# Sketched attention with a tanh-shrink layer on one core: key and query projections and the fold in larger matmuls, weights cast on other engines

## The chip, the core and the metric

The kernel runs on one core of a Trainium2 chip. Its engines run side by side, each with its own queue in program order: TensorE (PE; the loading of its weights, PEld, has a row of its own in the profile), VectorE (DVE), ScalarE (ACT), GpSimd (POOL) and SyncE (SP), which here only issues transfers. The metric is the device time of one execution in microseconds (us). A smaller number is better.

## The reference, cut to what matters

```python
# q, k, v: (4 batches, 4 heads, 1088 tokens, 32), S1, S2: (8, 32)
def phi(x):                                # 64 features for a token
    a = einsum('rd,bhsd->bhsr', S1, x)
    b = einsum('rd,bhsd->bhsr', S2, x)
    return (a[..., :, None] * b[..., None, :]).reshape(*x.shape[:-1], 64)
q_p, k_p = phi(q), phi(k)
kv = einsum('bhsf,bhsd->bhfd', k_p, v)
z = k_p.sum(axis=2)
num = einsum('bhsf,bhfd->bhsd', q_p, kv)
den = einsum('bhsf,bhf->bhs', q_p, z)[..., None] + 1e-06
x = (num / den)   # heads side by side: (4352 tokens, 128)
h = x @ w_in      # w_in: (128, 2048)
out = (h - tanh(h)) @ w_out               # w_out: (2048, 128)
```

## The kernel before, in words

**Planner.** The body does not issue instructions. `Program.op` (L74) records an operation with its engine, an assumed cost, the buffers it reads and writes, a priority and, for PE, a `mode` (which tile shape of the array it uses) and a count `ni` of instructions. `schedule` (L128) lists the operations in an order for each engine, `sync` (L226) puts the semaphore waits in, and `emit` (L290) writes the five queues. So the constants at L31 to L48, the costs and the priorities decide the order in which each engine takes its work; a wait at the head of a queue holds up all that stands behind it.

**Attention, batch by batch.** The first batch is cut into a chunk `a` of 512 tokens and a chunk `c` of 576; the others are one chunk each. The steps of a batch, with the lines of the profile:

- keys are loaded (L449) and turned by DVE (L547); PE projects them on both sketches (L565: for each 128 tokens two float32 matmuls of 64 tokens each, mode `k`); ACT and DVE copy them out (L575); POOL and DVE multiply out the 64 features (L583, L590);
- PE sums features times values, one 32-column tile for a head (L616), and a small Gram matrix of the sketches (L606), both in mode `kv`; DVE masks the Gram matrix (L634), PE folds S1 and S2 into it (L642, eight float32 matmuls in 32-column tiles), and the result goes beside the query sketch in `wq` (L649), so that the denominator comes out of the query projection; the sums are spread, turned and stored as `ndw` (L653, L659, L664);
- queries are loaded and turned (L465, L671); PE projects them (L700: four matmuls of 64 rows by 64 tokens for each 128 tokens, mode `q`); DVE goes through the denominator, its reciprocal and the products (L712 to L733, with POOL's half at L728) and turns the features (L739); PE weighs them with `ndw` in 32x32 tiles (L754, mode `nd`); DVE writes the result as bfloat16 into `xT` (L766, L772).

**Layer.** For each group of 512 tokens (eight, and a last one of 256), 16 times: PE multiplies `xT` by a 128-column block of `w_in` (L838), ACT takes tanh(-h) out of PSUM into a slot of `tt` (L841, 56 slots), PE adds tt times a block of `w_out` to an accumulator (L849). The linear term h @ w_out is x times the product w_in @ w_out, which is made once (L797, L802, L809, L813, L814) and added as a high and a low bfloat16 part (L830). DVE turns the accumulator (L856) and SP issues four transfers for each piece of the output (L865).

**Opening.** `load_w_in` and `load_w_out` are issued on SP straight behind the first batch's loads (L469, L473), in float32. `casts` makes them bfloat16: one quarter of `w_in` on ACT, three on POOL, both halves of `w_out` on POOL (L781, L786). `warm` (L510) gives PE matmuls on a zero tile to fill its gaps until the first chunk has been weighed. What sets the order around the change: SP's queue (k, v, q, then weights, then the next batch behind gates), ACT's queue up to the first tanh, and PE's queue, in which L797, L700 of chunk c and L754 of chunk a stand between the sums and the first L838. The gates at L39 name the step of a batch after which the next batch's k, q and v loads may be issued.

Of the kernel before, what the change touches and what calls it, by code (L numbers as in the profile page):

```python
# [12 lines left out]
R = 8  # L13
# [20 lines left out]
COPY_K = ("scalar", "scalar", "vector")  # L34
COPY_U = "vector"
COPY_Z = "scalar"
COPY_W = "scalar"
W_PRIO = 14
GATES = "kab", "x", "qp"  # L39
# [3 lines left out]
STRETCH = {"tensor": 1.3, "scalar": 1.3, "vector": 3, "gpsimd": 1.3, "sync": 1}  # L43
PASSES, HOLD, HELD = 6, 1.3, ("vector",)
FILL = 0.6
WARM = 4000
PACKET, FETCH, AHEAD = 256, 4500, 56
# [3 lines left out]
class Op:  # L51
    __slots__ = ("ni", "want", "eng", "cost", "fn", "deps", "order", "prio", "sem", "mode", "kids", "need", "ready", "at", "end", "idx", "know", "waits", "inc", "val")

    def __init__(self, eng, cost, fn, prio, sem, mode, want, ni):
        self.want, self.ni = want, ni
# [8 lines left out]
class Program:  # L64


    def __init__(self, nc):
        self.nc = nc
        self.ops = []
        self.writer = {}  # L70
        self.readers = {}
        self.last_fill = None

    def op(self, eng, cost, fn, r=(), w=(), prio=None, sem=None, mode=None, want=None, ni=2):  # L74
# [17 lines left out]
        for k in r:  # L92
            if k not in w:
                self.readers.setdefault(k, []).append(o)
        self.ops.append(o)
# [8 lines left out]
    def rank(self):  # L104
# [14 lines left out]
        for o in reversed(topo):  # L119
# [5 lines left out]
            if o.prio is None:  # L125
                o.prio = t / 1000
# [11 lines left out]
    def listed(self, seen):  # L138
# [21 lines left out]
        count, packets = 0, [0, 0]  # L160
# [11 lines left out]
        while left:  # L172
            best = None
            for e in engines:
# [3 lines left out]
                o = min((o for o in avail[e] if when(o) <= t + 20), key=lambda o: (o.prio, o.idx))  # L178
# [4 lines left out]
            fill = o.prio == 5000  # L183
# [12 lines left out]
            if o is self.last_fill:  # L196
                rest = [x for x in avail[e] if x.prio == 5000]
                left -= len(rest)
                avail[e] = [x for x in avail[e] if x.prio != 5000]
            o.at = when(o)  # L200
            dma = o.sem is not None
            if e == "tensor":
                if o.mode != mode:
                    o.at, mode = o.at + MODE, o.mode
                if (count + AHEAD) // PACKET != (count + o.ni + AHEAD) // PACKET:
                    packets.append(o.at + FETCH)
                count += o.ni
            cost = o.cost * 2 if e == "tensor" and o.at < WARM else o.cost
            if dma:
                bus = max(bus, o.at + 1500) + o.cost  # L210
                free[e], o.end = o.at + ISSUE, bus + 500
# [133 lines left out]
def bass_polysketch_attn__then__act_tanh_shrink_kernel(nc, q, k, v, S1, S2, moe_w_in, moe_w_out, out):  # L345
# [22 lines left out]
    pmask = sb("pmask", [128, 2])  # L368
    bmask = sb("bmask", [128, H])
    cmask = sb("cmask", [128, H])  # L370
    s_raw = sb("s_raw", [16, D])
    sel = sb("sel", [16, 16, R])
    s2c = sb("s2c", [128, H, D])
    wkm = sb("wkm", [128, 2, H, R])
    wq = sb("wq", [128, B, 2, 24])
# [3 lines left out]
    qT = [sb(f"qT{i}", [128, S]) for i in range(2)]  # L379
# [16 lines left out]
    w_out_f = sb("w_out_f", [128, NJB, DM])  # L396
# [45 lines left out]
    def load_small():  # L442
        load("scalar", 1024, ("s_raw",), "s", -3000, lambda e: e.dma_start(out=s_raw[0:8, :], in_=S1), True)
        load("scalar", 1024, ("s_raw",), "s", -3000, lambda e: e.dma_start(out=s_raw[8:16, :], in_=S2), True)
# [23 lines left out]
    def load_w_in(x, prio):  # L468
        load("sync", 262144, ("w_in_f", x), f"wi{x}", prio, lambda e: e.dma_start(  # L469
            out=w_in_f[:, 512 * x:512 * x + 512], in_=moe_w_in[:, 512 * x:512 * x + 512]))  # L470

    def load_w_out(x, prio):
        load("sync", 524288, ("w_out_f", x), f"wo{x}", prio, lambda e: e.dma_start(  # L473
            out=w_out_f[:, 8 * x:8 * x + 8, :].rearrange("p (x j) c -> p x (j c)", x=2),
            in_=moe_w_out.rearrange("(x ji jb) c -> ji x (jb c)", x=4, jb=4)[:, 2 * x:2 * x + 2, :]))


    def constants():
# [9 lines left out]
        for i in range(2):  # L488
            P.op("gpsimd", 100, lambda e, i=i: e.memset(kT[i][:, 8, 2:4, :], 0.0), w=[("kT0", i)], prio=-2980)
        P.op("gpsimd", 150, lambda e: e.memset(vx[0][64:128, :, 8, :], 0.0), w=[("vx0", 0)], prio=-2970)  # L490
# [3 lines left out]
        for r in range(2):  # L494
# [5 lines left out]
            out=pmask[:, :], in0=hmask[:, 0:2], in1=hmask[:, 2:4], op=ALU.add), r=[("hmask",)], w=[("pmask",)], prio=-2800)  # L500
        P.op("gpsimd", 150, lambda e: e.tensor_copy(
# [459 lines left out]
```

## Time and profile before

| | us |
|---|---|
| three runs | 115.69, 117.2, 121.72 |
| median of the runs | 117.2 |
| the profiled execution, device time | 114.97 |
| its span in the profile | 113.2 |
| PE busy / weight loads / DVE / ACT / POOL | 98.3 / 53.3 / 60.4 / 78.2 / 26.3 |
| first tanh starts | 20.98 |
| last tanh phase (no batch left to prepare) starts | 84.66 |
| last PE matmul group (L849 x16) starts | 107.22 |
| last DVE turn ends, then the last transfers | 109.68 |

PE's 3165 recorded rows (1573 matmuls and 1592 weight loads) come from its instruction stream; a float32 matmul leaves two matmul rows and two weight-load rows, a bfloat16 one leaves one of each. The granted clock is 1.0 in every stretch. In a row of the timeline the columns are start, length, engine, line, operation, output and inputs, count, and in brackets the idle time before it and what ended it; "issue" means that the profile shows nothing that it waited for.

### The profile page before, as it was taken

Reading aid. Unit: us, or ns where it says so; the run is one execution under the profiler, and the core shown is the slowest. Engines: PE = TensorE matmul, PEld = TensorE weight load, DVE = VectorE, ACT = ScalarE, POOL = GpSimd, SP = SyncE. Lnnn points to the kernel's source line nnn. Section 1 sums busy time; section 2 is a strip of 40 time slices with the busy share of each in tenths; the row PEclk is TensorE's granted clock in tenths of the full one; section 3 lists DMA queues with packets and bytes.
Section 4 is the critical chain, followed back from the end, with each engine's and each line's share of the span. In section 5 each row is a group of like instructions: output and inputs, shape, how many; then the busy total and the mean of one; then the engine's idle time right before and its main releaser. Section 6 shows DMA issues by size and latency. Waiting matters only on the chain.

```text
span 113.2 us, 3618 instructions
## 1 busy us (share of the span) xinstructions
PE 98.3 (87%) x1573; PEld 53.3 (47%) x1592; DVE 60.4 (53%) x115; ACT 78.2 (69%) x160; POOL 26.3 (23%) x34
## 2 busy tenths in 40 slices
PE   5999195699999996898999999799999999989950
PEld 2467174265556442546643464564444434435540
DVE  4677722997637996639399374739953020020210
ACT  4021251987766980797599669749979999999900
POOL 6352796400710150260025007002400000000000
PEclk9999999999999999999999999999999999999999
DMA  3988999300420505991000657060004114014062
GB/s 101 278 229 249 322 414 254 87 10 0 97 112 0 93 3 163 155 335 41 6 0 6 176 99 212 6 97 1 0 12 69 18 19 73 0 26 67 0 96 46
DMA packets 23663, 11.24 MB, mean 99 GB/s; under 512 B 18784, under 2 KB 21344, under 8 KB 23648
## 3 DMA queue, kind: packets, MB, share of 16 engines
q1 hardware_dynamic: 23616, 11.02, 38.7%
q8 instruction: 12, 0.20, 0.7%
q14 instruction: 3, 0.02, 0.1%
q10 hardware_dynamic: 32, 0.00, 0.0%
HBM read 8.78 MB, written 2.23 MB: 97 GB/s over the span
## 4 chain that ended last, share of the span: by engine, by line
PE 61%; ACT 11%; DVE 10%; DMA 7%; issue 6%; DVEq 0%
PE ps L849 16%; PE ps L838 15%; ACT tt L841 10%; PE ps L754 7%; PE ps L512 5%; PE ps L700 5%; DMA kraw<-in_k_dram 4%; DMA qraw<-in_q_dram 3%; PE ps L565 3%; PE ps L830 3%; DVE qpT L739 2%; PE ps L616 2%; DVE osb L856 2%; DVE qp L733 1%; PE ps L659 1%
## 5 line engine op out<-in xcount | busy, mean ns | idle before, releaser
L841 ACT ACTIVATE tt<-ps 128x512 bf16<-128x512 f32 (+1 forms) x144 | 70.0, 598 | 11.5 <-PE ps L754 6.6
L838 PE MATMUL ps<-xT,w_in 128*128 128x512 bf16 (+1 forms) x133 | 45.5, 368 | 3.4 <-DVE xT L766 1.1
L849 PE MATMUL ps<-tt,w_out 128*128 128x512 bf16 (+1 forms) x139 | 42.0, 367 | 0.2 <-issue 0.2
L838 PEld LDWEIGHTS ps<-xT,w_in 128*128 128x128 bf16 x144 | 13.1, 97 | 20.7 <-ACT tt L841 8.0
L849 PEld LDWEIGHTS ps<-tt,w_out 128*128 128x128 bf16 x144 | 14.1, 98 | 13.5 <-ACT tt L841 1.0
L856 DVE STREAM_TRANSPOSE osb<-ps 128x512 f32<-128x512 f32 (+1 forms) x9 | 6.1, 674 | 21.4 <-PE ps L849 15.0
L728 POOL TENSOR_TENSOR qp<-an,ab 128x1152 f32<-128x1152 f32 (+2 forms) x5 | 8.9, 1777 | 27.0 <-DVE an L724 26.8
L583 POOL TENSOR_TENSOR wk<-kab 128x512 f32<-128x512 f32 (+1 forms) x8 | 9.4, 1180 | 22.8 <-DVE kab L575 19.5
L739 DVE STREAM_TRANSPOSE qpT<-qp 128x1152 f32<-128x1152 f32 (+2 forms) x10 | 11.0, 1119 | 0.7 <-POOL qp L728 0.6
L754 PE MATMUL ps<-qpT,ndw 32*32 32x288 f32 (+3 forms) x320 | 7.3, 353 | 1.7 <-issue 1.2
L766 DVE CAST xT<-ps 128x512 bf16<-128x512 f32 x8 | 5.2, 682 | 5.8 <-PE ps L754 5.8
L512 PE MATMUL ps<-wz 128*128 128x512 bf16 x17 | 6.3, 484 | 1.7 <-DVE hmask L484 1.2
L671 DVE STREAM_TRANSPOSE qT<-qraw 128x512 f32<-128x512 f32 (+3 forms) x9 | 5.6, 658 | 4.0 <-DMA qraw<-in_q_dram 3.9
L547 DVE STREAM_TRANSPOSE kT<-kraw 128x256 f32<-128x256 f32 (+3 forms) x10 | 6.0, 612 | 3.0 <-DMA kraw<-in_k_dram 2.9
L616 PE MATMUL ps<-wk,vx 128*32 128x64 f32 x288 | 5.4, 221 | 2.4 <-issue 2.4
L754 PEld LDWEIGHTS ps<-qpT,ndw 32*32 32x32 f32 x320 | 4.2, 103 | 4.3 <-issue 1.7
L590 DVE TENSOR_TENSOR wk<-ps,kab 128x512 f32<-128x512 f32 (+1 forms) x8 | 5.7, 748 | 0.8 <-ACT kab L575 0.7
L700 PEld LDWEIGHTS ps<-wq,qT 64*64 64x64 f32 x320 | 5.2, 135 | 1.7 <-DVE wq L649 0.7
L700 PE MATMUL ps<-wq,qT 64*64 64x48 f32 (+2 forms) x320 | 5.9, 220 | 0.0
L616 PEld LDWEIGHTS ps<-wk,vx 128*32 128x32 f32 x288 | 4.4, 110 | 2.6 <-issue 2.5
L733 DVE TENSOR_TENSOR qp<-an,ps 128x1152 f32<-128x1152 f32 (+2 forms) x5 | 5.6, 1113 | 0.2
L575 ACT COPY kab<-ps 128x320 f32<-128x320 f32 (+1 forms) x5 | 2.1, 415 | 5.1 <-PE ps L565 5.0
(64 smaller groups left out, 66.2 us busy)
## 6 DMA issues: line engine op xcount, KB each, us to landing
kraw<-in_k_dram SPq DMA_DIRECT2D x3, 544.0 KB, 4.5
qraw<-in_q_dram SPq DMA_DIRECT2D x3, 544.0 KB, 4.1
out_dram<-osb SPq DMA_DIRECT2D x20, 64.0 KB, 2.0
w_in_f<-in_moe_w_in_dram SPq DMA_DIRECT2D x4, 256.0 KB, 5.0
w_out_f<-in_moe_w_out_dram SPq DMA_DIRECT2D x2, 512.0 KB, 8.3
vx<-in_v_dram SPq DMA_DIRECT2D x6, 144.0 KB, 3.0
vx<-in_v_dram SPq DMA_DIRECT2D x6, 128.0 KB, 3.3
vx<-in_v_dram SPq DMA_DIRECT2D x6, 64.0 KB, 2.7
```

The lines of the kernel that those rows point to most:

```text
L512: P.op("tensor", cost, lambda e: e.matmul(ps[:, 6, :], wz[:, 0:128], wz[:, :], start=True, stop=True), r=[("wz",)], prio=prio)
L583: P.op("gpsimd", pool(64 * n), lambda e, t0=t0, t1=t1, n=n, ab_=ab_: e.tensor_tensor(out=wk[:, 1, t0:t1, :, :].rearrange("p t h (i j) -> p ...
L616: ins = e.matmul(ps[32 * h:32 * h + 32, 2, 0:64], vx[i][:, h, t, :], wk[:, h // 2, t, h % 2, :], start=(t == 0), stop=(t == 8), tile_posit ...
L700: ins = e.matmul(dst[:, :, y0:y1], qT[i][64 * r:64 * r + 64, x:x + 64], wq[64 * r:64 * r + 64, b, :, y0:y1], start=True, stop=True, tile_p ...
L728: P.op("gpsimd", pool(64 * n), lambda e: e.tensor_tensor(out=qp[u][:, 1, 0:64 * n].rearrange("p (n i j) -> p n i j", i=R, j=R), in0=an[u][ ...
L733: P.op("vector", dve(64 * n), lambda e: e.tensor_tensor(out=qp[u][:, 0, 0:64 * n].rearrange("p (n i j) -> p n i j", i=R, j=R), in0=an[u][: ...
L739: P.op("vector", dve(64 * n), lambda e, r=r: e.transpose(out=qpT[u][:, r, 0:64 * n], in_=qp[u][:, r, 0:64 * n]), r=[("qp", u, r)], w=[("qp ...
L754: ins = e.matmul(ps[32 * h:32 * h + 32, k0 + s, 0:32 * own[s]], ndw[b % 2][32 * s:32 * s + 32, y, 32 * h:32 * h + 32], src, start=(y == 0) ...
L838: P.op("tensor", pe(n), lambda e, jb=jb, bk=bk: e.matmul(bk[:, 0:n], w_in[:, 128 * jb:128 * jb + 128], xT[:, t0:t0 + n], start=True, stop= ...
L841: P.op("scalar", act(n), lambda e, ts=ts, bk=bk: e.activation(out=tt[:, ts, 0:n], in_=bk[:, 0:n], func=AF.Tanh, scale=-1.0), r=[kb], w=[(" ...
L849: P.op("tensor", pe(n), lambda e, jb=jb, ts=ts: e.matmul(acc[:, 0:n], w_out[:, jb, :], tt[:, ts, 0:n], start=(jb == 0 and not g), stop=(jb ...
L856: P.op("vector", dve(n), lambda e: e.transpose(out=osb[u][:, 0:n], in_=acc[:, 0:n]), r=[ka], w=[("osb", u)], want=due(NJB) + LAG)
```

## The change

Parts on the data path:

1. **Projections and fold.** The key projection takes 128 tokens as one weight tile (9 matmuls a batch, 64 columns out, no tile position) where it took two of 64. The query projection takes 128 tokens: in the first batch with all 128 rows at once (`whole`, 96 columns out, a masked copy `wqb` of the sketch), in the others in two halves of 64 rows by 128 tokens (`halves`). The fold is two matmuls with 128 columns where it was eight with 32, and the sketch itself is spread with one matmul where it took four, S1 and S2 being loaded four times side by side for that. `qT` gets 64 zeroed columns.
2. **w_out** is loaded by two transfers on POOL's own queue that cast to bfloat16 on the way, behind POOL's product of chunk a; its float32 buffer and its two casts on POOL are gone, and its rows lie in another order (rows of 512 bytes in HBM).
3. **w_in** is issued on SP only after the first Gram matrix has been masked (`gm`); its four casts are all on ACT, with the same order of columns on both sides.
4. **Opening x** of chunk a is copied out of PSUM by ACT instead of DVE; the two `w_inT` copies go from ACT to DVE, and these turns of `w_in` use banks 0 and 2.
5. **Small moves.** In the later batches both key copies and the copy of the folded sketch are on ACT. The last group's four output transfers are issued two by SP and two by ACT. Gram and sums of the later batches are two operations. The first fill of PE is 40 matmuls of 64 columns, then 512-column ones. The q and v loads of the next batch have earlier gates.
6. **Planner.** Other constants, an instruction-fetch model with another start, and a rule that PE stays in a tile mode while it has work in it. So the order in every queue differs.

The diff, cut to its core:

```diff
-COPY_K = ("scalar", "scalar", "vector")
-COPY_U = "vector"
+COPY_K = ("scalar", "scalar", "scalar")
+COPY_U = "scalar"
-COPY_W = "scalar"
-W_PRIO = 14
-GATES = "kab", "x", "qp"
+COPY_W = "vector"
+W_PRIO = 30
+W_IN = -600, -599
+W_OUT = 9, 9
+BURN = 40
+X_A = "scalar"
+GATE_IN = ("gm",)
+GATE_OUT = ("qp", 0, 1)
+GATES = "kab", "qp", "an"
...
-STRETCH = {"tensor": 1.3, "scalar": 1.3, "vector": 3, "gpsimd": 1.3, "sync": 1}
-PASSES, HOLD, HELD = 6, 1.3, ("vector",)
+STRETCH = {"tensor": 1.3, "scalar": 1.3, "vector": 2.2, "gpsimd": 1.6, "sync": 1}
+PASSES, HOLD, HELD = 6, 0.6, ("vector",)
...
-PACKET, FETCH, AHEAD = 256, 4500, 56
+PACKET, FETCH, SLOW, BUSY = 256, 3200, 4500, 18000
...
-                o = min((o for o in avail[e] if when(o) <= t + 20), key=lambda o: (o.prio, o.idx))
+                o = min((o for o in avail[e] if when(o) <= t + 20), key=lambda o: (e != "tensor" or mode is None or o.mode != mode, o.prio, o.idx))
...
+    def load_w_in():
+        for x in range(4):
+            load("sync", 262144, ("w_in_f", x), f"wi{x}", W_IN[x // 2], lambda e, x=x: e.dma_start(
+                out=w_in_f[:, 512 * x:512 * x + 512], in_=moe_w_in[:, 512 * x:512 * x + 512]), gate=GATE_IN)
+            P.op("scalar", act(512) + 60, lambda e, x=x: e.copy(
+                w_in[:, 512 * x:512 * x + 512], w_in_f[:, 512 * x:512 * x + 512]),
+                r=[("w_in_f", x)], w=[("w_in", x)], prio=C_PRIO)
+
+    def load_w_out():
+        for x in range(2):
+            load("gpsimd", 524288, ("w_out", x), f"wo{x}", W_OUT[x], lambda e, x=x: e.dma_start(
+                out=w_out[:, 8 * x:8 * x + 8, :],
+                in_=moe_w_out.rearrange("(j p) c -> p j c", p=128)[:, 8 * x:8 * x + 8, :]), gate=GATE_OUT)
...
+        P.op("vector", dve(64), lambda e: e.tensor_tensor(
+            out=wqb[:, :, :, 0:16], in0=acc[:, None, None, 0:16].to_broadcast([128, 2, 2, 16]),
+            in1=hmask[:, :].rearrange("p (r h) -> p h r", h=2)[:, :, :, None].to_broadcast([128, 2, 2, 16]), op=ALU.mult),
+            r=[ka, ("hmask",)], w=[("wab",)])
...
                 for t in range(t0, t1):
-                    for c in range(2):
-                        ins = e.matmul(dst[64 * c:64 * c + 64, :, :, t - t0, :],
-                                       kT[i][:, t, 2 * c:2 * c + 2, :].rearrange("p c j -> p (c j)"),
-                                       wkm[:, :, :, :].rearrange("p x h i -> p (x h i)"),
-                                       start=True, stop=True, tile_position=(0, 64 * c))
+                    ins = e.matmul(dst[:, :, :, t - t0, :], kT[i][:, t, :, :].rearrange("p c j -> p (c j)"),
+                                   wkm[:, :, :, :].rearrange("p x h i -> p (x h i)"), start=True, stop=True)
...
             for y in range(2):
-                for h in range(H):
-                    ins = e.matmul(ps[32 * h:32 * h + 32, gb, 64:80], s2c[:, h, :],
-                                   gm[:, 2 * y:2 * y + 2, :].rearrange("p h i -> p (h i)"), start=(y == 0), stop=(y == 1),
-                                   tile_position=(0, 32 * h))
+                ins = e.matmul(ps[:, gb, 64:80], s2c[:, :, :].rearrange("p h d -> p (h d)"),
+                               gm[:, 2 * y:2 * y + 2, :].rearrange("p h i -> p (h i)"), start=(y == 0), stop=(y == 1))
...
+            def whole(e):
+                for t in range(nt):
+                    x = 32 * c.c0 + 128 * t
+                    dst = ps[:, k0, 96 * t:96 * t + 96].rearrange("p (h y) -> p h y", h=4)
+                    ins = e.matmul(dst[:, :, y0:y1], qT[i][:, x:x + 128],
+                                   wqb[:, :, :, y0:y1].rearrange("p h r y -> p (h r) y"), start=True, stop=True)
                 return ins
+            def halves(e):
+                for t in range(nt):
+                    x = 32 * c.c0 + 128 * t
+                    for r in range(2):
+                        dst = ps[:, k0 + r, 48 * t:48 * t + 48].rearrange("p (h y) -> p h y", h=2)
+                        ins = e.matmul(dst[:, :, y0:y1], qT[i][64 * r:64 * r + 64, x:x + 128],
+                                       wq[64 * r:64 * r + 64, b, :, y0:y1], start=True, stop=True,
+                                       tile_position=(64 * r, 0))
+                return ins
+            return halves if b else whole
...
-            P.op("vector", dve(128 * (z - a)), lambda e, a=a, z=z: e.tensor_copy(
+            eng = X_A if c.x == 0 else "vector"
+            P.op(eng, (dve if eng == "vector" else act)(128 * (z - a)), lambda e, a=a, z=z, eng=eng: (e.tensor_copy if eng == "vector" else e.copy)(
...
-                P.op("sync", 128 * w / 250, lambda e, b=b, c=c, m=m, cb=cb, at=done: e.dma_start(
+                P.op("scalar" if g == len(groups) - 1 and cb % 2 else "sync", 128 * w / 250, lambda e, b=b, c=c, m=m, cb=cb, at=done: e.dma_start(
...
-    warm(60, 216, 5000)
+    warm(BURN, 64, 29, 4999)
+    warm(60, 512, 216, 5000)
...
-    for x in range(4):
-        load_w_in(x, -790)
-    load_w_out(0, -760)
-    load_w_out(1, -750)
     sketch()
-    casts()
...
     k_back(0, a)
-    q_front(a, 0, early=True)
+    load_w_in()
+    q_front(a, 1, early=True, ab_eng=AB_A)
+    load_w_out()
```

## The prediction, as it was put on record

> **What bounds the kernel now.** I read the page's busy shares first, then the chain, then the timeline of ACT, because the layer's 144 tanh are all there.
>
> ```profile
> PE 98.3 (87%) x1573; PEld 53.3 (47%) x1592; DVE 60.4 (53%) x115; ACT 78.2 (69%) x160; POOL 26.3 (23%) x34
> ...
> q8 instruction: 12, 0.20, 0.7%
> ...
> PE 61%; ACT 11%; DVE 10%; DMA 7%; issue 6%; DVEq 0%
> ```
>
> PE has most of the chain, but 6% of it, some 7 us, is "issue". ACT's timeline:
>
> ```profile
> 20.98 2.56 ACT L841 ACTIVATE tt<-ps 128x512 bf16<-128x512 f32 x5
> ...
> 45.91 1.57 ACT L841 ACTIVATE tt<-ps 128x512 bf16<-128x512 f32 x3 [3.82 <-PE ps L754]
> ...
> 84.66 18.61 ACT L841 ACTIVATE tt<-ps 128x512 bf16<-128x512 f32 x38 [0.81 <-PE ps L754]
> ```
>
> There are three stages. Up to 20.98 nothing of the layer runs. From there to 84.66 ACT starves whenever the next batch's x is late (3.82 before batch 1's, at 45.91): the chain of a batch (keys, sums, queries, DVE, weighing) sets the pace, with PE nearly full. From 84.66 ACT is full at 18.61/38 = 0.49 a tanh. PE's timeline says why the first stage is long:
>
> ```profile
> 13.62 0.41 PE L616 MATMUL ps<-wk,vx 128*32 128x64 f32 x11 [2.37 <-issue]
> ...
> 19.07 0.41 PE L754 MATMUL ps<-qpT,ndw 32*32 32x128 f32 x4 [1.19 <-issue]
> ```
>
> PE stops twice in the middle of one operation, with data there. Counting PE's rows in its order, matmuls and weight loads, 442 lie ahead of the first stop and 255 between the two. Queue q8 brought 12 packets for about 3,200 rows. So I read the stops as instruction fetches of 256 rows that are late: if each is asked for when the one before is entered, the two took 13.62 - 8.65 = 5.0 and 19.07 - 13.62 = 5.45.
>
> **The change part by part.**
>
> *Fetches.* With the new order, 428 rows stand ahead of the first weighing. The edge at 442 falls into its first half, the edge at 698 into chunk c's weighing at about 23. A fetch asked for at row 186 (about 9.0) is in by 14.5, and the weighing starts at 15.3. Both stops go; what covers the fetch is 0.8 us.
>
> *Price of a 128-column float32 weight tile.* This is the largest unknown. The rows of the shapes replaced, and the one row of a full float32 tile (L659, a transpose):
>
> ```profile
> 46.23 1.13 PEld L565 LDWEIGHTS ps<-wkm,kT 128*64 128x64 f32 x36 [0.42 <-DVE xT L766]
> ...
> 52.90 0.22 PEld L642 LDWEIGHTS ps<-gm,s2c 128*32 128x32 f32 x16 [0.69 <-DVE gm L634]
> ...
> 53.14 0.20 PEld L659 LDWEIGHTS ps<-ident,kvz 128*128 128x128 f32 x2
> ```
>
> One L565 load lasts 0.138 and one of L659 0.14, so the starts are (1.13 - 0.138)/35 = 0.028 apart, and the chain shows 1.20 for the 36 rows, 0.033 each. In L659 the second load starts 0.20 - 0.14 = 0.06 after the first. Lower bound: 64 columns stream in 0.053 (two L565 rows, side by side, take 0.056 to 0.066). Upper bound: columns per ns fall with the number of column tiles, 32/0.0073 with four (L642: (0.22 - 0.112)/15), 64/0.028 with two; halved again, one full tile takes 0.111. I take 0.066, twice L565's row, because L659 is the only row of the shape itself. Then a key projection is 18 x 0.066 = 1.19 against 1.20; queries (two row tiles side by side) 36 x 0.033 = 1.19 against 1.24 (L700); the fold 4 x 0.066 = 0.26 against 0.25. So no gain and no loss. The Trainium skill (TensorE: Matmul & The Clock Gate, LDWEIGHTS) says that a weight load takes its columns divided by 1.2 GHz, whatever the rows, and that its fast load leaves out float32. That is 0.107 for 128 columns: it speaks against this change and for the upper bound, and by it the sum is that of rival 1.
>
> *Opening, walked along the new queues with the durations of the trace.* The sketch arrives at 4.28 as before. The 40 short fills must be over by then: at 0.06 each from 1.19 they are (L809 runs 16 matmuls in 0.89, 0.056 each); at half the clock, seen in 0.43 for a 512-column fill, 0.11 each, they would cost 1.7. PE: key projection 5.95 to 6.5 and 6.9 to 7.6, four fills, Gram 8.8, sums 9.4, a/b projection 9.9, fold 10.2, four fills, second projection 11.6, chunk c's 10 rows of 96 columns at 0.085 to 12.4, second sums 13.0. DVE: an is ready 1.3 after 11.75 (as from 10.75 to 12.03), qpT at 14.8 and 15.8. ACT: chunk c's copy until 12.9, then casts and copies in turn (cast, kvz 0.38, cast, ndw 0.37, cast, cast). A cast took 1.09 with scattered columns; with columns in order I take 0.6, the tanh of the same shape, so w_in is ready at 16.05. Its four transfers start at 9.3 instead of 6.38; the first quarter took 4.6 in a busy queue, so 13.9 at worst, 1.0 behind ACT's place for it, and this is in the range. PE: first turn of w_in 15.2, weighing 15.3 to 16.4, second turn 16.85. The x copy on ACT (0.37 for 256 columns, 0.42 for 320, so 0.57) ends at 17.1, the first tanh starts at 17.65: 3.3 earlier. With casts at 1.09 it would be 19.2. The two w_inT copies cost DVE 1.2 each (1.35 for 1152 columns) and are covered: chunk c's features are ready at 21.4, its weighing comes at about 23.
>
> *What reaches batch 1.* PE now needs nine tanh and the product ahead of chunk c's weighing: that ends at 24.5 and the key projection at 26.95, against 29.00: 2.0 earlier. The other 1.3 is lost again, as ACT waits for batch 1's x.
>
> *Batches.* Key projection and fold no longer switch the tile mode: four switches less a batch at about 0.1 (L565 starts 0.09 behind its turn at 27.73): 0.4 x 3 = 1.2. Two waits go: the mask of Gram stood behind a key turn that waited for its transfer (0.69 idle ahead of L642 at 52.90, above), 0.6; and batch 3's queries were late:
>
> ```profile
> 71.23 1.37 DVE L671 STREAM_TRANSPOSE qT<-qraw 128x576 f32<-128x576 f32 x2 [2.15 <-DMA qraw<-in_q_dram]
> ```
>
> Their gate now opens at the turned features instead of xT, so 1.0 of this comes back (the sums ended at 72.2, the projection began at 74.11). The copies moved to ACT, 0.37 + 0.17 a batch, lie in its starved time; without that cover 1.6.
>
> *Tail.* The last four output transfers take SP some 0.45 each behind the last turn; with two on ACT 0.8 is saved.
>
> *w_out.* Its 2.2 of casts on POOL go. The first transfer is issued behind POOL's product, at 14.2. PE's queue stops for it at the first L849, at 19.5, and for the second at the product, at 21.3; behind both stand all L838, so ACT starves too. No row shows a transfer issued by POOL. Lower bound: SP's issue, 0.45; upper: 8.3 for each, w_out's own time to landing now. With k, q and w_out, 2.15 MB at the 0.39 MB/us of 14 to 18 us, the second lands near 20.7. I take no stall.
>
> Sum against the profiled execution: 2.0 + 1.2 + 0.6 + 1.0 + 0.8 = 5.6, so 114.97 - 5.6 = 109.4. That execution lies 1.9% below the median of the runs (117.2), of which it would leave 111.6. I forecast 111.0, between the two.
>
> **The rivals.**
>
> 1. *Full float32 tiles load at 0.111.* For: the fall from four column tiles to two. Against: L659. Each batch gets 18 x 0.045 = 0.8 for keys, 36 x 0.023 = 0.8 for queries, 0.2 for the fold, in a chain that ACT waits for: 5.3 in three batches; the opening's 16 + 18 + 10 such rows add 1.9. Time 109.4 + 7.2 = 116.6, on the median's scale 118.8: slower than before. It decides from 0.101 a row, where 5.6 is used up.
> 2. *w_out late.* At 8.3 for each, one behind the other, the second lands at 30.8, 9.5 behind its place: 118.9. It overturns the gain from a landing at 26.9. For: POOL's queue makes 1,024 short rows for each transfer and its next product waits behind; against: the same queues moved 0.41 MB/us in 14 to 16. The Trainium skill (DMA: Bandwidth & Descriptors, Anatomy of one DMA) gives a POOL-issued transfer 2.0 us plus bytes over 436 GB/s, 3.2 for 0.5 MB, an estimate that no run here shows yet; by it there is no stall.
> 3. *The opening keeps its stops.* The fetch takes 7.8, as the k load did in that stretch, and PE stops for 1.4 in the weighing, or the fills or casts cost their upper bounds. The first tanh is at 19.1 to 19.4 and batch 1's chain gains some 0.5 instead of 2.0: 110.9, on the median's scale 113.1.
>
> **How the numbers follow.** Forecast 0.60, rival 1 0.17, rival 2 0.10, rival 3 0.13. Low end: PE's work from the first L838 at 17.2 is about 82.3 (272 full L838 and L849 at 0.2157 make 58.7, the linear part 3.7, weighing 6.0, sums and Gram 4.1, keys 3.6, queries 3.6, product, turns and folds 2.6); with 2.5 for the switches left and 114.97 - 109.14 - 0.8 = 5.0 behind the last matmul this gives 107.0, and with float32 rows at 0.053 1.7 less, 105.3. High end: 118.8 and 118.9 of the rivals. About 2% can be told from no change in this kernel. Faster by more: the forecast less 0.02 and most of rival 3, 0.68; within 2%: much of rival 1, 0.18; slower: 0.14, rival 2 and the rest of rival 1.
>
> **What would show it.** No idle row of PE marked "issue" above 0.5 up to 20; first tanh between 17 and 18.5; a key projection of 1.1 to 1.3 in the chain (2.0 means rival 1); w_out landing by 19.5 and 21.3; 45.91 at about 44; at most 0.5 of waiting for qraw. I am wrong if the full tiles cost over 0.1 a row or the first L849 waits for a transfer.

## The result, and the profile after

The changed kernel takes 124.65 us in the median of six runs (121.78 to 131.27); the kernel before, beside it, 117.76 (115.69 to 123.33). The ratio, taken over the undisturbed runs of both, is 1.0485, with a 95% interval of 1.0368 to 1.0602: the change makes the kernel slower by some 5%, and the forecast of 111.0 us was wrong. Times of both kernels spread by several us, mainly through their opening, so I compare profiles by stretches. The profiled execution of the changed kernel takes 121.78 us (span 120.0, before 113.2). First the lines of its page that answer to those shown of before: the busy time of the engines, the granted clock of TensorE in tenths over 40 slices of 3 us, two transfer queues, and the chain's shares.

```profile
PE 107.8 (90%) x1304; PEld 64.8 (54%) x1320; DVE 59.8 (50%) x113; ACT 79.8 (67%) x167; POOL 23.2 (19%) x33
...
PEclk9999999967999999999999999999999999999999
...
q0 software_dynamic: 2080, 0.52, 4.6%
q8 instruction: 10, 0.16, 0.7%
...
PE 72%; DMA 9%; DVE 9%; ACT 3%; issue 2%; POOL 1%; ACTq 0%; DVEq 0%
```

PE has 541 rows less and is 9.5 us busier; transfers went from 7% to 9% of the chain, issue from 6% to 2%; and the clock, 1.0 throughout before, dips around 25 us. ACT's timeline of the changed kernel, columns as before:

```profile
19.08 3.05 ACT L866 ACTIVATE tt<-ps 128x512 bf16<-128x512 f32 x6 [0.48 <-PE ps L820]
24.40 1.72 ACT L866 ACTIVATE tt<-ps 128x512 bf16<-128x512 f32 x3 [2.27 <-PE ps L863]
28.54 1.57 ACT L866 ACTIVATE tt<-ps 128x512 bf16<-128x512 f32 x3 [2.42 <-PE ps L863]
...
50.90 1.57 ACT L866 ACTIVATE tt<-ps 128x512 bf16<-128x512 f32 x3 [4.78 <-PE ps L786]
...
91.95 18.68 ACT L866 ACTIVATE tt<-ps 128x512 bf16<-128x512 f32 x38 [0.93 <-PE ps L786]
```

The first tanh is 1.9 earlier (19.08 against 20.98). Batch 1's tanh, at 45.91 before, comes at 50.90; the last phase, at 84.66 before, at 91.95. So a lead of 1.9 has become a lag of 5.0 within one batch, and grows by 2.3 in the next two. PE's timeline and the chain of waits show two causes:

```profile
16.82 1.15 PE L786 MATMUL ps<-qpT,ndw 32*32 32x128 f32 x64
...
23.54 0.60 PE L874 MATMUL ps<-tt,w_out 128*128 128x512 bf16 x2 [2.44 <-DMA w_out<-in_moe_w_out_dram]
...
26.34 1.87 PE L834 MATMUL ps<-w_out,w_inT 128*128 128x128 bf16 x16
```

```profile
31.60 1.96 PE ps L588 x18
...
37.90 0.55 PE ps L660 x4
...
39.11 2.17 PE ps L730 x36
```

The chain of waits of the kernel before has these rows for the same steps of batch 1 (L565 keys, L642 fold, L700 queries):

```profile
27.80 1.20 PE ps L565 x36
...
34.20 0.25 PE ps L642 x16
...
35.04 1.24 PE ps L700 x72
```

The weighing (L786) runs through where L754 stopped for 1.19. At 21.1 PE is ready for w_out and waits 2.44 us; the product (L834), whose row lasts 1.06 before, takes 1.87. And the wide tiles of batch 1 take 1.96 for keys (18 rows), 2.17 for queries (36) and 0.55 for the fold (4), where the chain before had 1.20, 1.24 and 0.25 to 0.32: 0.109, 0.060 and 0.14 a row.

### The profile page after: what moved, and what is told of

It is laid out like the page before. It is cut to its first block, busy times and chain, and to the rows that moved or that the text cites. A ratio compares the mean times of both kernels' runs of the same rounds, so it can differ in the third digit from the quotient of the medians.

```text
span 120.0 us, 3074 instructions
## 1 busy us (share of the span) xinstructions
PE 107.8 (90%) x1304; PEld 64.8 (54%) x1320; DVE 59.8 (50%) x113; ACT 79.8 (67%) x167; POOL 23.2 (19%) x33
## 3 DMA queue, kind: packets, MB, share of 16 engines
q0 software_dynamic: 2080, 0.52, 4.6%
## 4 chain that ended last, share of the span: by engine, by line
PE 72%; DMA 9%; DVE 9%; ACT 3%; issue 2%; POOL 1%; ACTq 0%; DVEq 0%
PE ps L874 20%; PE ps L863 20%; PE ps L588 7%; DMA w_out<-in_moe_w_out_dram 6%; PE ps L730 5%; PE ps L786 5%; ACT tt L866 3%; PE ps L855 3%; PE ps L637 3%; DMA s_raw<-in_S_dram 3%; PE ps L537 2%; DVE qpT L771 2%; PE ps L660 2%; DVE osb L881 2%; PE ps L834 2%
## 5 line engine op out<-in xcount | busy, mean ns | idle before, releaser
L874 PE MATMUL ps<-tt,w_out 128*128 128x512 bf16 (+1 forms) x142 | 42.8, 371 | 2.6 <-DMA w_out<-in_moe_w_out_dram 2.4
L863 PEld LDWEIGHTS ps<-xT,w_in 128*128 128x128 bf16 x144 | 13.7, 101 | 19.9 <-ACT tt L866 7.2
L588 PEld LDWEIGHTS ps<-wkm,kT 128*128 128x128 f32 x72 | 8.7, 192 | 1.0 <-DVE xT L800 0.6
L588 PE MATMUL ps<-wkm,kT 128*128 128x64 f32 x72 | 8.7, 273 | 0.0
L537 PE MATMUL ps<-wz 128*128 128x64 bf16 (+1 forms) x57 | 7.2, 287 | 1.5 <-DVE hmask L504 1.2
L596 ACT COPY kab<-ps 128x256 f32<-128x256 f32 (+1 forms) x8 | 3.2, 399 | 7.0 <-PE ps L588 7.0
L786 PE MATMUL ps<-qpT,ndw 32*32 32x288 f32 (+3 forms) x320 | 6.9, 352 | 0.9 <-DVE qpT L771 0.9
L744 DVE COPY ab<-ps 128x576 f32<-128x576 f32 (+1 forms) x4 | 2.7, 674 | 8.3 <-PE ps L730 7.5
L800 DVE CAST xT<-ps 128x512 bf16<-128x512 f32 x7 | 4.6, 687 | 4.5 <-PE ps L786 4.5
L730 PEld LDWEIGHTS ps<-wq,qT 64*128 64x128 f32 x108 | 6.3, 188 | 0.8 <-ACT wq L673 0.4
L730 PE MATMUL ps<-wq,qT 64*128 64x48 f32 x108 | 6.6, 274 | 0.0
L786 PEld LDWEIGHTS ps<-qpT,ndw 32*32 32x32 f32 x320 | 4.0, 103 | 3.6 <-DVE qpT L771 1.8
```

The source lines that it names most:

```text
L537: P.op("tensor", cost, lambda e: e.matmul(ps[:, 6, 0:cols], wz[:, 0:128], wz[:, 0:cols], start=True, stop=True), r=[("wz",)], prio=prio)
L588: ins = e.matmul(dst[:, :, :, t - t0, :], kT[i][:, t, :, :].rearrange("p c j -> p (c j)"), wkm[:, :, :, :].rearrange("p x h i -> p (x h i) ...
L730: ins = e.matmul(dst[:, :, y0:y1], qT[i][64 * r:64 * r + 64, x:x + 128], wq[64 * r:64 * r + 64, b, :, y0:y1], start=True, stop=True, tile_ ...
L786: ins = e.matmul(ps[32 * h:32 * h + 32, k0 + s, 0:32 * own[s]], ndw[b % 2][32 * s:32 * s + 32, y, 32 * h:32 * h + 32], src, start=(y == 0) ...
L863: P.op("tensor", pe(n), lambda e, jb=jb, bk=bk: e.matmul(bk[:, 0:n], w_in[:, 128 * jb:128 * jb + 128], xT[:, t0:t0 + n], start=True, stop= ...
L874: P.op("tensor", pe(n), lambda e, jb=jb, ts=ts: e.matmul(acc[:, 0:n], w_out[:, jb, :], tt[:, ts, 0:n], start=(jb == 0 and not g), stop=(jb ...
```

## The experiments

The table gives, for the profile of each run, the first tanh and the stretch from there to the end of the span. The second number depends little on how fast the opening ran, except where PE waits for w_out or its clock falls behind a wait. "Wide" and "narrow" are the tiles of batches 1 to 3; "late" is w_out's place in the changed kernel.

| kernel | first tanh | from there to the end |
|---|---|---|
| before | 20.98 | 92.2 |
| before, profiled again (e13) | 23.40 | 92.8 |
| before with wide tiles (e10) | 21.71 | 97.2 |
| before with 42 rows more (e11) | 21.59 | 92.3 |
| after: wide, late | 19.08 | 100.9 |
| e1: narrow, late | 24.88 | 98.9 |
| e2: wide, early | 25.00 | 96.7 |
| e3: wide, late, wait filled | 24.45 | 100.4 |
| e4: narrow, early | 29.55 | 92.0 |
| e5: wide, late, fills ahead | 18.73 | 105.5 |
| e8: as e5, opening narrow | 18.07 | 109.2 |
| e6, e7: narrow, early, fills ahead | 20.34, 23.11 | 95.1, 91.9 |
| e9: wide, late in 2 KB rows, fills ahead | 20.49 | 98.1 |
| e14: all narrow, late, fills ahead | 17.97 | 96.3 |
| e12: all narrow, earliest, fills ahead | 19.14 | 91.7 |

**The wide tiles.** My theory: they load at 0.11 a row and lie on the path. The rival: w_out alone did it. `e1_narrow_batches` undoes the tiles where b is not 0 (cut to its core; the fold likewise):

```diff
+NARROW = lambda b: b > 0
...
+                    for c in range(2 if NARROW(b) else 0):
+                        ins = e.matmul(dst[64 * c:64 * c + 64, :, :, t - t0, :],
...
+                    if NARROW(b):
+                        continue
...
-                    for r in range(2):
...
+                    for s, r in [(s, r) for s in range(2) for r in range(2)]:
...
-                                       tile_position=(64 * r, 0))
+                                       tile_position=(64 * r, 64 * s))
```

> The changed kernel, but in batches 1 to 3 the key projection is again two tiles of 64 columns, the query projection four of 64 by 64, and the fold eight of 32 columns; every instruction keeps its place, and the opening keeps its wide tiles. Theory A (the wide float32 tiles are loaded at 0.11 us and lie on the path): key rows of a batch go from 1.96-2.04 us back to about 1.2, query rows from 2.15 to about 1.25, fold from 0.55 to about 0.3, so some 1.9 us a batch; chunk c's weighing stays at 29.3, batch 1's tanh after x at 50.9 moves to about 49, the last phase from 91.95 to 86-88, the span from 120.0 to 115-116. Rival B (w_out's late landing alone; the wide tiles lie in time that TensorE would wait anyway): the rows shrink as much, but the span stays within 119-120.5.

`e10_before_wide` does the one part alone in the kernel before (the same lines the other way round):

> The kernel before with only one part of the change: in batches 1 to 3 the key projection in tiles of 128 columns, the query projection in tiles of 64 by 128 (the last of nine left narrow), and the fold in one of 128 columns; each instruction group in its old place. Theory A (a 128-column float32 load costs 0.11 against 0.066 for two of 64 columns, and lies on the path): +1.7 to 1.9 us a batch, last phase at 89.8-90.4 instead of 84.66, span 118.3-119 against 113.2. Rival B (in the old order there is slack that takes it): span 113-115.5.

ACT's timeline of e1, the tanh that follow on the x of batches 1, 2 and 3:

```profile
58.45 1.57 ACT L880 ACTIVATE tt<-ps 128x512 bf16<-128x512 f32 x3 [4.78 <-PE ps L877]
...
76.70 2.07 ACT L880 ACTIVATE tt<-ps 128x512 bf16<-128x512 f32 x4 [1.11 <-PE ps L877]
...
95.74 18.69 ACT L880 ACTIVATE tt<-ps 128x512 bf16<-128x512 f32 x38 [0.93 <-PE ps L877]
```

The steps are 18.25 and 19.04, against 20.13 and 20.92 after: 1.88 less each, as expected. The span as such (123.8, times 117.89 to 125.56) says nothing, since this profile's opening ran at half speed and w_out made PE wait 4.76; both are taken up below. In e10 the stretch behind the first tanh grows by 5.0, one step from 19.37 to 21.31, the next from 19.38 to 20.68, one from 24.93 to 26.64. Its times give only 1.0199 [1.0118, 1.0279], because those of before lay at 117.4 and more beside it. So I profiled before again:

> The kernel before, unchanged, with a profile from this study's chip, beside its many times there of 117.4 and more against 115.0 in the first profile. Theory A (only the opening varies from run to run): from the first tanh on the profile is the same as the first one's within 0.3 us (24.93 us to batch 1's tanh, 19.37, 19.38, and 28.5 behind it), and the first tanh comes later than 20.98 where the fills of 512 columns take 0.43 us longer than in the first profile or the two stops are longer. Then the wide tiles' price in the kernel before is the 4.95 us that its stretches behind the first tanh show, not the 2.4 us of the comparison of times. Rival B (the stretches behind the first tanh vary by 1 us or more too): then 4.95 is too much.

```profile
14.69 0.41 PE L616 MATMUL ps<-wk,vx 128*32 128x64 f32 x11 [3.38 <-issue]
```

Here its first stop took 3.38 instead of 2.37, PE ran at half speed for 3.4 us behind it (15.3 to 18.8), and the first tanh came at 23.40. Behind that it needed 24.93, 19.74 and 19.56: the first step is that of the first profile, the others are 0.37 and 0.18 longer, one a little over the 0.3 that I allowed. So e10 prices the tiles at 4.5 to 5.0. The same kernel against itself gave a ratio of 1.024 [1.003, 1.046] there: differences of 2% in these times alone prove little.

**The place of w_out.** `e2_wout_early` and `e4_both` (e1 and e2 together) move its transfers on POOL's queue:

```diff
+        pq = order["gpsimd"]
+        wo = [o for o in pq if o.sem in ("wo0", "wo1")]
+        for o in wo:
+            o.deps = set()
+            pq.remove(o)
+        pq[16:16] = wo        # behind the two wk products
```

> The changed kernel with w_out's two transfers moved on GpSimd's queue from behind the first qp product to behind the two wk products (issue at about 10 instead of 15.7), and not held by that product. Theory A (late landing, and the halved clock that follows TensorE's wait): both halves land by about 20, the wait of 2.44 us ahead of the first use at 21.1 goes and with it the clock of 0.50 from 25 to 28; chunk c's weighing moves from 29.3 to 24-25.5, the span from 120.0 to 114.5-116. Rival B (the transfer engines are full in 10 to 25 us, so earlier only displaces others): w_in or batch 1's loads land later by as much, first tanh moves from 19.1 to 20 or later, span 117.5-120. Rival C (the clock falls for another reason): the wait goes, the clock still falls between 24 and 29, span about 117-117.5.

> The narrow tiles in batches 1 to 3 and w_out's early transfers together. Theory A (both parts lie on the path and add): span 110-112, below the 113.2 of the kernel before, since the opening keeps its lead of 1.9 us and the tail its 0.5. Rival B (one of them is hidden by the other): span no better than the better of the two alone, 114.5 or more.

In e2 the stretch behind the first tanh is 4.2 shorter than after: PE has no wait for w_out. But its rival B was right for the opening: w_in's quarters took up to 7.9 to land instead of 4.6, ACT's casts waited 3.2 for them, and PE 2.13 ahead of the second turn of w_in. In e4 both parts add up to 92.0, as little as before. Its best time was 115.46, so no run came down to the span of 110 to 112 that theory A gave; in the profile the opening ran at half speed.

`e14_narrow_wout_late` isolates the place with a fast opening, against e12 below; it has the edits of e1 (in every batch), e8 and e5, and w_out where the change puts it:

> Narrow tiles everywhere and the three fills ahead, but w_out's transfers at the changed kernel's own place, behind the first qp product: against the all-narrow run only w_out's place differs. Theory A (late landing costs the wait and the halved clock behind it): first tanh at 18.1, w_out's first half lands at 24-27 as in the two runs before with this opening, TensorE waits 4-7 us, clock 0.50 for some 3 us behind it, span 116-118.5 against 110.9. Rival B (the wait is hidden, since TensorE has slack behind it): span 111-113.

```profile
22.86 1.04 PE L899 MATMUL ps<-tt,w_out 128*128 128x512 bf16 x2 [2.87 <-DMA w_out<-in_moe_w_out_dram]
```

The span is 114.2 instead of 110.9, between the ranges of the two theories, and the stretch behind the first tanh is 4.6 longer; 1.2 of it comes back in the opening, where e12 waits for the queries of batch 0, which land beside w_out (below). The wait of 2.87 fell short of the 4 to 7 expected; the clock was 0.50 from 22.6 to 26.1.

**The clock.** After PE's wait the granted clock is 0.50 for one stretch. Windows of the changed kernel (the columns are the stretch's length, busy us of PE, PEld, DVE, ACT and POOL with the instructions, then granted clock, transfer share, GB/s):

```profile
24.00:24.50 0.50, 0.50 (x4) 0.26 (x3) 0.00 (x0) 0.10 (x1) 0.00 (x0) 1.00 1.11 220
24.50:25.00 0.50, 0.50 (x4) 0.26 (x3) 0.00 (x0) 0.50 (x2) 0.00 (x0) 0.83 0.96 193
25.00:25.50 0.50, 0.50 (x3) 0.16 (x2) 0.00 (x0) 0.48 (x1) 0.00 (x0) 0.50 0.47 76
...
28.00:28.50 0.50, 0.50 (x4) 0.25 (x3) 0.26 (x1) 0.00 (x0) 0.00 (x0) 0.76 0.00 0
```

It falls at about 24.8, 1.3 after PE has resumed, and returns at 28.2. `e3_fills_in_wait` gives PE work in the wait (`first` is the first matmul that reads w_out):

```diff
+        fills = [Op("tensor", 216, self.dummy, 0, None, None, None, 2) for _ in range(11)]
...
+        tq[first:first] = fills
...
+    P.dummy = lambda e: e.matmul(ps[:, 1, 0:512], wz[:, 0:128], wz[:, 0:512], start=True, stop=True)
```

> The changed kernel with 11 matmuls of 512 columns on the constant tile wz put into TensorE's queue between the sixth first-layer matmul and the first matmul that uses w_out, so that TensorE works (2.4 us) through its wait; nothing else is moved, and w_out lands as late. Theory A (the clock of 0.50 from 25 to 28 follows from TensorE's idle time): the clock stays at 1.0, the 16 product matmuls take 0.9 instead of 1.87 us, the wait up to 23.5 is filled, span 118.0-118.6. Rival B (the clock falls by what is running then, not by the wait before): the clock still falls, span 119.8-120.5.

```profile
PEclk9999999999999999999999999999999999999999
```

The clock stays at 1.0 in every slice: theory A holds for the cause. But behind the first tanh it gains only 0.5, since the product then waits 1.22 for w_out's second half. The halved clock had mostly covered time in which that half was not there. The span, 124.9, again carries a slow opening.

**The opening.** In e1 to e4 the fills of 512 columns took 0.43 instead of 0.216 until 10.9 us (e2) to 26 us (e4). All four had one thing in common: the sketch landed at 4.8 to 5.1 instead of 4.4, and PE stood idle for 0.8 to 1.1 ahead of it, the 40 short fills being over at 3.9. `e5_fills_ahead` moves three fills ahead of the sketch's matmuls:

```diff
+        a, z = [x for x, o in enumerate(tq) if o.prio < 4999][:3:2]
+        move = [o for o in tq[a:z] if o.prio >= 4999]
+        tq[a:z] = move + [o for o in tq[a:z] if o.prio < 4999]
```

> The changed kernel with three of its 512-column fills moved from behind the two sketch matmuls to ahead of them, so that TensorE stays busy until about 5.2 us, past the landing of s_raw (4.4 in the profile of the changed kernel, 4.8 to 5.1 in the runs of this study). Theory A (TensorE runs at half speed until it has worked without a pause; the 40 short fills end at 3.9, and a pause of 0.8 to 1.1 us ahead of the sketch kept the opening at half speed up to 10-26 us): the fills' matmuls fall from 0.43 to 0.216 us each by about 6 us in every run, the first key copy ends by 7.5, first tanh at 19-19.7, the time is 121.5-123 in every run, without the 127 to 131 of some runs. Rival B (the slow openings come of something else, such as later landings of k and q): fills of 0.43 us beyond 8 us still occur, times still spread over 5 us or more.

```profile
24.77 1.03 PE L878 MATMUL ps<-tt,w_out 128*128 128x512 bf16 x2 [4.02 <-DMA w_out<-in_moe_w_out_dram]
...
52.50 3.94 PE L592 MATMUL ps<-wkm,kT 128*128 128x64 f32 x18
```

The first tanh came at 18.73 and the fills at 6.2 ran at full speed, as theory A has it; the time did not follow: 125.74 to 128.69 (1.0726 [1.0624, 1.0827]). The wait is 4.02: PE was ready for w_out 0.35 sooner, and the first half landed 9.4 after its issue instead of 7.8. The clock fell twice, from 24.4 to 27.8 and from 51.8 to 58.5. The second fall made the step from batch 1's tanh to batch 2's 23.38 instead of 20.13; 18 key rows took 3.94 in it. What set it off was not tried. It is in e6 (48.6 to 52.0) and e8 (53.7 to 60.5) too. Of the seven kernels with the fills ahead, six ran at full speed by 7.1, the seventh (e7) only by about 13.5, with no pause to be seen. The chip does not decide it, since e14, taken on the chip of e1 to e4, is among the six. So the pause favours a slow opening and is not all of it.

`e6_both_fills_ahead` and `e7_wout_earlier` add the fills to e4; e7 puts w_out ahead of the wk products (`pq[14:14] = wo`):

> The same three fills moved ahead in the kernel with narrow tiles in batches 1 to 3 and w_out's transfers behind the wk products. Theory A: the opening at full speed by 6 us, 18.25 and 18.9 us from batch to batch as in the run without the fills ahead; the sum 19.1 to 20.5 (first tanh, up to 1.5 later because w_in shares the transfer engines with w_out) + 26.8 + 18.25 + 18.9 + 28.1 = 111-112.6 span, 113-114.4 us. Rival B: w_in, whose transfers are slowed to 6-8 us by w_out's beside them, lands after 20, and first tanh comes at 21.5-22.5: span 113.5 to 114.5, as the kernel before.

> As the run before it in this group, but w_out's two transfers stand ahead of the two wk products on GpSimd's queue (issue at about 3 to 5 us, beside batch 0's own loads). Theory A (w_out is then out of w_in's way, and batch 0's loads leave room): w_in lands 3.5-5 us after its issue, first tanh by 19.5, span 110.5-111.5. Rival B (the transfer engines are the bound in the opening): batch 0's q and v land later, the key and query work wait for them, first tanh at 20-22, span 112-114.

e6: 113.23 at best, 116.57 in the median. Its w_in was late again (PE idle for 1.59 ahead of the second turn), and the first tanh came at 20.34, still inside theory A's range. The span of 115.4 in the profile lies above both theories, as the clock was 0.50 from 21.3 to 24.7 and fell a second time; that of the fastest run, 111.4, lies in theory A's range. e7: 113.15 at best; w_in landed in 3.1 to 4.1 and nothing waited for w_out, as theory A has it, but its opening was the slow one.

**Why w_out is late.** After: 2,080 packets on q0 take 4.6% of 16 engines' span, 42 ns each, for 256 bytes; the packets of q1 take 30 ns for 440 bytes on average. `e9_wout_2kb_rows` reads four rows of w_out at once:

```diff
-                in_=moe_w_out.rearrange("(j p) c -> p j c", p=128)[:, 8 * x:8 * x + 8, :]), gate=GATE_OUT)
+                in_=moe_w_out.rearrange("(x ji jb) c -> ji x (jb c)", x=4, jb=4)[:, 2 * x:2 * x + 2, :]), gate=GATE_OUT)
...
+                w_in[:, 512 * x:512 * x + 512].rearrange("p (jb ji) -> p jb ji", jb=4),
```

> The changed kernel with the three fills moved ahead, and w_out read as in the kernel before, in rows of 2 KB (four rows of w_out to a partition at once) instead of 512 bytes; the cast by the transfer, its issue and its place stay; w_in's columns are permuted to match by ScalarE's casts. Theory A (the small packets make w_out late: 2,048 packets of 256 bytes at 42 ns each are 86 us of the 16 engines, beside batch 1's loads): a quarter of the packets, landing 5-6.5 us after the issue at 15.4-16.4 instead of 9.4-10.9; TensorE's wait ahead of the first use falls from 4.0 to 0-1.5 us, the clock of 0.50 behind it goes, span 116-118.5 against 124.2 for the same kernel with small rows. Rival B (batch 1's loads or GpSimd's own pace bound it): landing 8-11 us again, span 122-125.

```profile
22.90 0.60 PE L879 MATMUL ps<-tt,w_out 128*128 128x512 bf16 x2 [0.38 <-DMA w_out<-in_moe_w_out_dram]
...
25.77 1.05 PE L839 MATMUL ps<-w_out,w_inT 128*128 128x128 bf16 x16 [0.76 <-DMA w_out<-in_moe_w_out_dram]
```

```profile
q0 software_dynamic: 544, 0.52, 3.2%
```

Those are PE's timeline and the queue's row on the page. The waits are 0.38 and 0.76 and the span is 118.6, 0.1 above A's range (times 1.0219 [1.0143, 1.0295] of before), but not for A's reason alone. The landing fell only from 9.4 and 10.9 to 6.8 and 8.7, and ACT's casts with scattered columns took 1.15 instead of 0.62, so that PE needed w_out later. Packets are part of the cause; what share GpSimd's own pace and batch 1's loads have stays open.

**The stops of the kernel before.** `e8_opening_narrow` (e5 with narrow tiles in the opening alone) was to bring them back:

```diff
+NARROW = lambda b: b == 0
...
+                    for s in range(2 if NARROW(b) else 0):
...
+                        ins = e.matmul(ds[:, :, y0:y1], qT[i][:, x + 64 * s:x + 64 * s + 64],
...
+                                       tile_position=(0, 64 * s))
```

> The changed kernel with the three fills moved ahead, and in the opening alone the key and query projections again as two tiles of 64 columns and the fold as eight of 32: some 112 more instruction rows ahead of the first weighing, as many more as lie between the stop of the kernel before and its place. Theory A (the kernel before stopped in the opening, 2.37 and 1.19 us, because instruction packets of 256 rows had not come): idle time that ends in nothing but issue, of 1 us or more, is back on TensorE between 9 and 19 us, and first tanh at 20-21.5 though the key and query rows are 1-1.5 us shorter in sum. Rival B (the stops had another cause): no issue idle over 0.3, first tanh at 17.8-18.5.

No stop came, and the first tanh was at 18.07, 0.66 earlier than in e5, as rival B has it. By count the 440 rows of the kernel before's first stop end early in the second sums, reached at 13.1 there and at 11.25 before: too late to tell the theories apart. (PE waited 6.80 for w_out, the longest of all, and the times were 123.82 to 129.32.) `e11_before_rows` is the better test:

```diff
+        for o in order["tensor"][:3]:
+            o.fn = self.short              # eight matmuls of 64 columns instead of one of 512
```

> The kernel before with its first three 512-column fills each replaced by eight of 64 columns (the same time, 42 instruction rows more ahead of everything). Theory A (the stops of TensorE, 2.37 us behind the 29th of 40 records of the second sums group and 1.19 us behind the 60th of 64 of the first weighing, are the edges of instruction packets of 256 rows): both stops move back by 42 rows, that is 21 records: to about the 8th of 40 and the 39th of 64, with about the same length. Rival B (they belong to what is computed there, or to a transfer): they stay at the 29th and the 60th.

```profile
10.40 0.32 PE L625 MATMUL ps<-wk,vx 128*32 128x64 f32 x8
13.30 0.65 PE L625 MATMUL ps<-wk,vx 128*32 128x64 f32 x32 [2.58 <-issue]
...
19.45 0.64 PE L763 MATMUL ps<-qpT,ndw 32*32 32x128 f32 x25 [0.34 <-issue]
```

Behind the 8th of 40 and the 39th of 64: to the record as foretold. The first stop is as long as expected (2.58 for 2.37), the second only 0.34 instead of 1.19; PE reached it later, its clock having been 0.50 from 14.7 to 18.1. The place of the stops belongs to the count of instructions.

The kernels with narrow tiles in the batches have such stops too, in batch 1's query projection (e4; at the same record for 0.34, 1.21 and 0.71 in e1, e6 and e7) or in batch 2's (e12; 0.34 in e14). PE's timelines of e4 and e12:

```profile
46.14 0.55 PE L750 MATMUL ps<-wq,qT 64*64 64x48 f32 x21 [0.88 <-issue]
```

```profile
53.93 0.57 PE L761 MATMUL ps<-wq,qT 64*64 64x48 f32 x25 [0.69 <-issue]
```

Weight-load rows ahead of the stops: 221 and 349 in the kernel before, e11 and e13, 604 in e1, e4, e6 and e7, 988 in e12 and e14. With a matmul to each load the distances, 128, 255 and 384, are one, two and three times 256 rows, within a row.

**The best of the parts.** `e12_all_narrow`: narrow tiles everywhere, the fills ahead, `pq[14:14] = wo`; the rest of the change is kept.

> The best of the parts: narrow tiles in every batch and in the opening, the three fills ahead, w_out's cast transfers ahead of the wk products; the rest of the change (fewer mode switches, w_in's casts and x's copy on ScalarE, the tail) is kept. Theory A (parts add): against the run with wide tiles in the opening, 0.6 us earlier first tanh (18.07 against 18.73 with and without narrow tiles in the opening), 91.9 us behind the first tanh: span 110.0-111.0, 111.8-112.8 us, 3-4% below the kernel before. Rival B (in the opening the time saved goes into waits for w_in or for instructions): 113 us as the run before it.

```profile
12.67 1.51 PE L747 MATMUL ps<-wqb,qT 128*64 128x32 f32 x36 [1.37 <-DVE wqb L690]
...
20.99 0.59 PE L905 MATMUL ps<-tt,w_out 128*128 128x512 bf16 x2
```

112.64 to 114.46 us, 0.9583 [0.9534, 0.9632] of before: 4% faster, and better than both kernels. PE takes w_out up at 20.99 without a wait. The 0.6 earlier first tanh did not come (19.14): batch 0's second query load now takes 5.7 to land, beside w_out, DVE waits 2.43 for it, and the masked sketch that PE needs stands behind that turn: PE waits 1.37.

## Why the prediction was wrong

The sum of 5.6 gained stands against 6.8 lost in the profiled executions. Behind the first tanh the change costs 8.7 (100.9 against 92.2): the wide tiles 4.7 (e2 against e4; 4.5 to 5.0 in the kernel before), w_out's lateness 4.2 (after against e2; 4.6 in e14 against e12, but 6.9 in e1 against e4, where PE waited 4.76). Together 8.9, so all other parts come to about zero there. That zero hides two things: e4 has a stop for instructions in batch 1 that the wide tiles do not have, some 1.2 (below), so the tiles as such cost 5.9; and the rest of the change then gains some 1.4.

- **Price of the wide tile: the step that failed first.** I took 0.066 a row, from two loads of a transpose that start 0.06 apart. The key projection shows 0.109 to 0.113, my upper bound. A pair of loads says how close two may start, not what a long run of them sustains; the fall from four to two column tiles, which I had worked out, was the right row. Rival 1 gave 5.3 in three batches; e1 shows 1.88 in each of two, and the three come to 4.7 against e4, 5.9 without its stop. The Trainium skill (TensorE: Matmul & The Clock Gate, LDWEIGHTS) had it: 128 columns at 1.2 GHz are 0.107, and this trace agrees (0.109 to 0.113).
- **w_out: the second.** I had the second half landing near 20.7, from the MB to be moved, and no stall. The issue came at 15.70, 1.5 later than walked; the halves landed 7.8 and 9.4 behind their issues, at 23.5 and 26.1, the first 2.4 behind its need. My upper bound of 8.3 for a transfer was nearly right, but I chained two of them for rival 2 and gave it 0.10. The Trainium skill's fit (DMA: Bandwidth & Descriptors, Anatomy of one DMA) gives 3.2; this trace disagrees (7.8 and 9.4). That both rivals could hold at once I had not counted; each alone I had put at 118.8 or 118.9. The 118.9 stands on the scale of the profiled execution; on that of the median, as rival 1's, it is 121.2, so the high end was too low by my own sum.
- **Fetches: right.** No issue idle over 0.16 up to 20, q8 down from 12 packets to 10; e11 moved the stops by count. With narrow tiles in the batches the rows come back, q8 has 12 packets, and a stop is back in batch 1 or 2.
- **Opening: half right.** First tanh 19.08, not 17.65, yet 1.9 earlier. Casts 0.62 (0.6), x copy 0.59 (0.57). The tiles added 0.66 (e5 against e8), rival 1 had said 1.9. That the clock itself is at stake I missed.
- **"2.0 reaches batch 1": wrong.** Even in e4, with narrow tiles and no wait for w_out, the stretch from first tanh to batch 1's is 26.80 against 24.93, 1.9 longer. Of this, 1.2 is e4's own stop: its query projection takes 2.40 in the chain, the 0.88 included, where e12, without a stop there, has 1.24 and needs 25.63 for the stretch. The other 0.7 is in e12 too. By the end of batch 1's query projection ACT has done 23 tanh in e7 and e12 and 21 in before, so the order puts more of the layer ahead of it; that this is the cause was not tried. In the changed kernel the stretch takes 31.82, 4.2 more than in e2 (27.65, w_out early), and e2 with its wide tiles takes 2.0 more than e12.
- **Mode switches: not seen.** Rows of 0.8, 0.9 and 0.27 a batch sum to 1.97; e1 gave 1.88 back although it has the switches again. So four switches cost some 0.1 a batch by this estimate, not 0.4.
- **Batch 2: more than forecast.** The step to batch 2's tanh is 18.25 in e1 and e4 against 19.37, 1.1 less, where I had 0.6 for the wait for Gram's mask; where the rest comes from stays open.
- **Batch 3's gate and the tail: about half.** The wait for qraw is gone and e4's last step is 18.90 against 19.38; the last phase to the end takes 28.0 instead of 28.5, where I had 0.8.

## What to carry to other kernels

Price a new tile shape from a long run of the nearest shape, and when two bounds lie a factor of two apart, let the one of the same kind of work decide. A transfer that moves to another queue has a new issue time and a new rate: walk both up to the instruction that needs it, and see what waits behind that one. Compare stretches between milestones when openings vary; a faster opening only helps if what is loaded behind it comes sooner too.

## What the runs showed of the hardware

- TensorE's clock halved for 3.4 us behind idle time, mostly while PE was already busy again: behind 2.44 of waiting in the changed kernel, 2.13 in e2, 1.59 with some gaps in e6 and a stop of 2.58 in e11. In e1 the wait was 4.76; the clock fell within it and stayed low for 6.8 (29.7 to 36.5). Filling the wait (e3) kept it at 1.0; but it also stayed at 1.0 in the kernel before, behind a stop of 2.37: the length of the idle time alone does not decide. The Trainium skill (TensorE: Matmul & The Clock Gate, Part 1) tells of free windows of 3.4 us and of an idle window ahead of the slow state; the length agrees, with two windows in e1, and the idle time needed was shorter here.
- In the opening the rows of granted clock show 1.0 while the fills take 0.43 instead of 0.216: the durations tell, not that row.
- 64-column float32 tiles side by side load in 0.033 a row, a full one in 0.11: the same 128 columns load 1.7 times as fast in two tiles (1.20 against 2.00 for a key projection).
- PE's stops for instructions lay whole multiples of 256 rows apart and lasted 0.34 to 3.38 us; not every such place brought one (e4 has none at 221 or 349 weight loads). The narrow tiles' extra rows cost e4 1.2 at such a place, which the wide tiles are spared.
